# A list schedule of all tasks orders every engine; the first two batches' group sums are added on the chip

## The chip, the cores and the metric

The kernel runs on one core of one Trainium2 chip. The metric is the time of one execution in device microseconds; where several runs were made, the median is given with the lowest and the highest.

## What is computed

The reference is an attention block followed by a gated feed-forward block, in float32. There are 8 batches, 8 heads, 576 positions and 64 values a head; the feed-forward block has 512 inputs and 1536 inner columns.

```python
q_d = q.reshape(B, H, Sd, 4, D).mean(axis=3)        # and k_d, v_d: groups of four positions
out_up = np.repeat(softmax_attention(q_d, k_d, v_d), 4, axis=2)
mask = np.abs(pos[:, None] - pos[None, :]) < 4      # a band of 7 positions
out_local = softmax(where(mask, q @ k.T / 8, -1e9)) @ v
x = (out_up + out_local) as (4608 tokens, 512)
xn = x / sqrt(mean(x * x) + 1e-6) * rms_g
out = (silu(xn @ w_gate) * (xn @ w_val)) @ w_out
```

So each token gets a **coarse** attention over 144 group means, a **band** attention over its 7 neighbours, and the feed-forward block.

## The kernel before

**Chunks.** The 4608 tokens are cut into 18 chunks of 256. A chunk's band attention runs on 128 partitions. VectorE multiplies queries by a window of keys (`score`, line 387) and sums over the head's 64 values (`score_sum`, line 393), in 8 pairs a chunk; then a small softmax (lines 403 to 430). The weights multiply the values on three engines: ScalarE (line 441), VectorE and GpSimd, called POOL in the profile (both line 450). Seven products are summed by VectorE (line 470) or, in chunks 0 and 1, by TensorE with products against an identity matrix (line 465). `load_up` and `add_up` (lines 479 and 487) read the coarse result from device memory and add it. Squares (ScalarE, line 493), a sum over partitions (TensorE, line 500) and a Newton iteration (VectorE at lines 521 to 523 in chunks 0 and 1, else POOL at 525 to 528) give the norm, which line 532 multiplies in. TensorE transposes (line 543), ScalarE takes the high part `xh` (line 545), VectorE the low part `xl` (line 549).

**Feed-forward.** The weights and activations are held as a high and a low part, and every product is three: high x high, low x high, high x low. `Inner` makes for each of 12 column groups f the gate and the value product (24 products of 256 columns, line 619), a tanh on ScalarE (line 625), two steps on VectorE (lines 628 and 633), the high part `hs` on ScalarE (line 638) and its low part (line 641), on POOL in chunks 0 and 1 and on VectorE after. `second` (line 600, six products of 512 columns) follows two f later (`LAG = 2`) and adds up in `ps_o`.

**Coarse items.** There are 64 heads, of which two make one `Coarse` item: 32 items, 8 for each pair of batches. Scores (line 264), a maximum (273), exponentials (281), transposes (293), copies (298), products with the values (303), a scaling (318), and a store to device memory (319). A chunk needs the 8 items of its pair of batches. The sums over groups of four positions are made by transfers: `sum_loads` loads the first addend and lets POOL issue three more for each of `qk` and `vs` with `accum_op=ALU.add` (line 237), each of which waits for the one ahead.

**Weight decoding.** The weights arrive as 64-bit values, in 36 pieces of 512 KB (line 161), since the host only reinterprets the arrays. Each piece goes through `scale` (ScalarE, line 165), `last_bits` (POOL at 175 or ScalarE at 173), `join` (VectorE, line 182), the high part (ScalarE, lines 190 and 192) and `split`, the low part (VectorE at 204, POOL at 200). The 24 pieces of the gate and value weights and 12 of the output weights go through four buffers `o_sb`. All this belongs to the opening and to chunk 0.

**What sets the order.** Until chunk 0 is done, generators ("lanes") yield times to a rough clock (`Clock`), and `run` takes the lane that is due: this order holds on VectorE, POOL and SyncE. From chunk 1 on, a list `todo` of steps with a place (f from 0 to 12) is worked off between the f of the chunk ahead; `COARSE` says how many coarse items go with a chunk (0, 4, 3, 1, then 2). TensorE and ScalarE get their order from the framework's own scheduler.

Of the kernel before, what the change touches and what calls it, by code (L numbers as in the profile page):

```python
# [86 lines left out]
def attn_moe_kernel(  # L87
# [131 lines left out]
    latest = []  # L219


    up_dram = {}
    sums = {}

    def sum_loads(b, half, engine=nc.sync):
        if b == 1:
            qk = xp.tile([P, 2, 2, SD], FP32, name=("xh", "xl")[half])
            vs = ffn.tile([HALF, 4, 2, D], FP32, name="hs", bufs=LAG + 1)
        else:
            qk = glob.tile([P, 2, 2, SD], FP32, name="qk")  # L230
            vs = glob.tile([HALF, 4, 2, D], FP32, name="vs")
        sums[b, half] = (qk[:, 0], qk[:, 1], vs)
        steps = []
        for j in range(FAC):
            for t, src in ((qk.rearrange("p t h n -> p (t h n)"), qk_sum), (vs.rearrange("p h c d -> p (h c d)"), v_sum)):
                if j:
                    steps.append(lambda t=t, src=src[b, j, :, half]: nc.gpsimd.dma_start(out=t, in_=src, accum_op=ALU.add))  # L237
# [831 lines left out]
```

## Time and profile before

| what | value |
|---|---|
| median of 3 runs (lowest to highest) | 1182.68 us (1181.16 to 1185.43) |
| the profiled execution | 1189.22 us |
| its span, first to last instruction | 1187.4 us |
| its mean granted TensorE clock | 0.957 |
| read from device memory, written | 106.33 MB, 11.80 MB |

Times in rows are microseconds from the span's start. A row of the timeline gives start, duration, engine, line, operation, the tiles (output <- inputs), shapes and count, and in brackets how long the engine was idle just before and what ended that. Rows by stage give for each engine the busy time and the number of instructions, then TensorE's granted clock (1.00 is full), the transfer engines' mean busy share and what they moved in GB/s. Groups by line give count, busy time, mean duration in ns, and idle time ahead. PE is TensorE, PEld its weight load, DVE VectorE, ACT ScalarE, SP SyncE; a q behind a name is the engine's sequencer. A product of float32 operands stands in the trace as two records, one of the rounded type `fp32r` as one.

### The profile page before, as it was taken

How to read it: one execution, taken by the hardware profiler on the slowest of the kernel's cores; microseconds unless marked ns; L12 is line 12 of the kernel's file. 1: busy time of each engine (PE TensorE's matmuls, PEld its weight loads, DVE VectorE, ACT ScalarE, POOL GpSimd, SP SyncE). 2: the span in 40 equal slices, each digit the busy share in tenths (PEclk: the TensorE clock that was granted, in tenths of full speed). 3: DMA queues.
4: the chain of work that ended last, by engine and by line, in shares of the span. 5: the costliest groups of instructions: out<-in, count | busy, mean ns of one | idle time of the engine just before them, and what ended most of it. 6: DMA issues, size and time to landing. Idle time of an engine off the chain costs nothing. (4 is left out here: it accounts for less than half of the span.)

```text
span 1187.4 us, 22113 instructions
## 1 busy us (share of the span) xinstructions
PE 1105.9 (93%) x7940; PEld 1015.3 (86%) x7940; DVE 905.0 (76%) x1732; ACT 610.1 (51%) x2233; POOL 306.5 (26%) x503
## 2 busy tenths in 40 slices
PE   1893996987999999999999999999999999999998
PEld 1683995887999998989898989899999999999997
DVE  5676888976878878787878787888897979886322
ACT  0455762536372846473737374747374563727221
POOL 3443745533132112222222222211112121111000
PEclk9557897998999999999999999999999999999999
DMA  9946638555635252525252525222221313220000
GB/s 246 231 144 184 225 125 181 128 114 110 129 76 121 69 122 72 123 76 119 75 121 79 116 78 118 80 64 78 57 86 54 102 43 104 60 62 19 1 19 18
DMA packets 77293, 119.56 MB, mean 101 GB/s; under 512 B 27264, under 2 KB 36736, under 8 KB 77184
## 3 DMA queue, kind: packets, MB, share of 16 engines
q1 hardware_dynamic: 47760, 91.12, 26.5%
q0 software_dynamic: 11520, 21.24, 11.0%
q10 hardware_dynamic: 17904, 5.80, 2.1%
q8 instruction: 62, 1.02, 0.4%
q14 instruction: 47, 0.39, 0.1%
HBM read 106.33 MB, written 11.80 MB: 99 GB/s over the span
## 5 line engine op out<-in xcount | busy, mean ns | idle before, releaser
L600 PE MATMUL ps_o<-wo,hs 128*128 128x512 f32 x1296 | 366.6, 403 | 17.6 <-POOL hs L641 7.9
L619 PE MATMUL ps_h<-xh,wg 128*128 128x256 f32 x1728 | 360.4, 286 | 6.6 <-DVE sil L633 5.8
L619 PE MATMUL ps_h<-xh,wv 128*128 128x256 f32 x1728 | 351.1, 283 | 1.0 <-DVE wv L204 1.0
L619 PEld LDWEIGHTS ps_h<-xh,wg 128*128 128x128 f32 x1728 | 288.4, 192 | 17.8 <-DVE sil L633 6.4
L619 PEld LDWEIGHTS ps_h<-xh,wv 128*128 128x128 f32 x1728 | 286.8, 192 | 4.4 <-DVE wv L204 1.2
L441 ACT ACTIVATE prod<-kv,sc 128x64 f32<-128x64 f32 x1024 | 271.1, 406 | 22.5 <-DVE sc L430 11.1
L600 PEld LDWEIGHTS ps_o<-wo,hs 128*128 128x128 f32 x1296 | 223.7, 191 | 56.9 <-POOL hs L641 10.4
L619 PE MATMUL ps_h<-xl,wg 128*128 128x256 f32 x864 | 247.7, 287 | 0.3 <-DVE xl L549 0.3
L619 PE MATMUL ps_h<-xl,wv 128*128 128x256 f32 x864 | 245.2, 284 | 0.0
L625 ACT ACTIVATE sil<-ps_h 128x256 f32<-128x256 f32 x216 | 82.6, 382 | 245.8 <-PE ps_h L619 238.0
L450 POOL TENSOR_TENSOR prod<-sc,kv 128x256 f32<-128x256 f32 x144 | 116.5, 848 | 252.2 <-ACT xh L545 63.7
L619 PEld LDWEIGHTS ps_h<-xl,wg 128*128 128x128 f32 x864 | 165.5, 192 | 8.3 <-DVE sil L628 1.2
L619 PEld LDWEIGHTS ps_h<-xl,wv 128*128 128x128 f32 x864 | 165.7, 192 | 1.8
L628 DVE SCALAR_TENSOR_TENSOR sil<-sil,ps_h 128x256 f32<-128x256 f32 x216 | 90.0, 417 | 99.2 <-ACT sil L625 98.7
L387 DVE TENSOR_TENSOR prod<-q_t,kv 128x896 f32<-128x896 f32 x140 | 156.3, 1118 | 7.4 <-DMA q_t<-in_q_band_dram 7.1
L638 ACT ACTIVATE hs<-sil 128x256 fp32r<-128x256 f32 x216 | 88.9, 414 | 136.7 <-DVE sil L633 121.5
L470 DVE TENSOR_REDUCE x_t<-prod 128x128 f32<-128x896 f32 x128 | 136.8, 1084 | 26.8 <-ACT prod L441 13.3
L393 DVE TENSOR_REDUCE sc<-prod 128x14 f32<-128x896 f32 x144 | 154.3, 1077 | 0.0
L641 DVE TENSOR_TENSOR hs<-sil,hs 128x256 fp32r<-128x256 f32 x192 | 80.7, 421 | 31.8 <-ACT hs L638 31.8
L237 POOL DMA_DIRECT2D qk<-in_qk_sum_dram x42 | 37.7, 898 | 224.5 <-DMA qk<-in_qk_sum_dram 165.0
L633 DVE SCALAR_TENSOR_TENSOR sil<-sil,ps_h 128x256 f32<-128x256 f32 x216 | 89.6, 415 | 2.0
L450 DVE TENSOR_TENSOR prod<-sc,kv 128x128 f32<-128x128 f32 (+3 forms) x144 | 75.2, 554 | 3.4 <-PE ps_o L465 2.3
(111 smaller groups left out, 1016.6 us busy)
## 6 DMA issues: line engine op xcount, KB each, us to landing
kv<-in_k_pad_dram SPq DMA_DIRECT2D x72, 320.0 KB
kv<-in_v_pad_dram SPq DMA_DIRECT2D x72, 320.0 KB
qk<-in_qk_sum_dram POOLq DMA_DIRECT2D x42, 288.0 KB, 5.6
out_dram<-o_sb SPq DMA_DIRECT2D x36, 256.0 KB
q_t<-in_q_band_dram SPq DMA_DIRECT2D x70, 128.0 KB
vs<-in_v_sum_dram POOLq DMA_DIRECT2D x42, 144.0 KB, 3.9
wg<-in_w_gate_dram SPq DMA_DIRECT2D x8, 512.0 KB
wg<-in_w_val_dram SPq DMA_DIRECT2D x8, 512.0 KB
```

What stands on the lines that cost most here:

```text
L387: engine.tensor_tensor(out=pr[:, :, a:b], in0=bcast(q[:, s0:s0 + 2], 2, b - a), in1=window(k, s0, a, b), op=ALU.mult,)
L393: nc.vector.tensor_reduce(out=self.sc[:, j, par, s0:s0 + 2], in_=self.pr[i], axis=AX.X, op=ALU.add,)
L441: nc.scalar.activation(out=pr[:, o, s], in_=self.v[j, par][:, s0 + s + o], func=AF.Copy, scale=p[:, s, o:o + 1],)
L450: engine.tensor_tensor(out=self.pr[i][:, a:b], in0=bcast(p[:, :, a:b].rearrange("p s o -> p o s"), 3, D), in1=window(self.v[j, par], s0, a ...
L470: nc.vector.tensor_reduce(out=self.x[j][:, s0:s0 + 2, par], in_=pr.rearrange("p o s d -> p s d o"), axis=AX.X, op=ALU.add,)
L600: nc.tensor.matmul(out=o_ps[c][j], lhsT=lhs[:, cols], rhs=rhs(f)[:, 0], start=(f == 0 and i == 0), stop=(f == NF - 1 and i == 2),)
L619: nc.tensor.matmul(out=hp_[:, t], lhsT=wi(f)[:, 0, k], rhs=xi[:, k], start=(n == 0), stop=(n == 3 * KT - 1),)
L625: nc.scalar.activation(out=self.sil, in_=hp_[:, 0], func=AF.Tanh, scale=0.5)
L628: nc.vector.scalar_tensor_tensor(out=self.sil, in0=self.sil, scalar=1.0, in1=self.p[:, 0], op0=ALU.add, op1=ALU.mult,)
L633: nc.vector.scalar_tensor_tensor(out=self.sil, in0=self.sil, scalar=0.5, in1=self.p[:, 1], op0=ALU.mult, op1=ALU.mult,)
L638: nc.scalar.activation(out=self.hh, in_=self.sil, func=AF.Copy)
L641: (nc.gpsimd if self.c in REST_P else nc.vector).tensor_tensor(out=self.hl, in0=self.sil, in1=self.hh, op=ALU.subtract,)
```

## The change

**A list schedule.** All work becomes tasks with an engine (or a choice of two), a cost, a due time, the tasks that go ahead and the buffers that are allocated and used. `Plan.run` keeps a clock for each engine; it takes the task that can start first, and among those of one engine that could start within 0.15 us the one with the earliest due time, emits it, and goes on. Buffers count: a task that allocates waits until the users of the buffer that it takes over are done in the plan. The order so found holds on all five engines, TensorE and ScalarE included. `due` gives chunk 0 the time 70, chunk 1 125, chunk 2 180, and then 57 or 52 for each.

**Sums on the chip.** For the first two batches all four addends are loaded side by side with plain transfers into places where weights come later (`OpeningSums`). TensorE adds the four of `qk` with products against the identity into PSUM, ScalarE copies them out; POOL or VectorE adds those of `vs`. The other batches keep the accumulating transfers (`Sums`), each issue now a task of its own on POOL.

**Also.** The low part of `hs` may go to VectorE or POOL in every chunk, whichever the plan finds earlier. Coarse stores and loads are all issued by ScalarE. Coarse items are spread by due times: those of batches 2 and 3 over chunks 1 to 3, of 4 and 5 over chunks 4 to 8, of 6 and 7 over chunks 9 to 12. The first products for warming are 30 in place of 32. Raw weight pieces use eight places of the later gate and value weights rather than four, and four of the output weights.

```diff
+    def run(self):
...
+                for t in tasks:
+                    at = self.room(t) if t.allocs else 0.0
+                    if at is not None:
+                        floor = free["DMA"] - 3.0 if t.dma else 0.0
+                        found.append((max(free[e], t.at, at, floor), t))
...
+                first = min(s for s, _ in found)
+                pick = min(
+                    ((next(o for o in t.options if o[0] == e)[2], t.n, s, t) for s, t in found if s <= first + NEAR),
+                    key=lambda x: x[:2],
+                )
+                if best is None or pick[2] < best[0]:
+                    best = (pick[2], e, pick[3])
...
+    due = [70.0, 125.0, 180.0]
+    for c in range(2, NCH):
+        due.append(due[-1] + (57.0 if c < 12 else 52.0))
...
+    class Sums:
...
+            for j in range(1, FAC):
+                for i in range(2):
+                    done[i] = task(
+                        "POOL", ISSUE, lambda i=i, j=j: self.more(i, j), at - 30 + 5 * j, [done[i]],
+                        uses=[(self.qk_buf, self.vs_buf)[i]], dma=(0.288, 0.144)[i] * MB * 1.7,
+                    )
...
+    class OpeningSums:
...
+            for t in range(2):
+                p = buf(tag)
+                add = task("PE", 2.3, lambda t=t: self.add(t), at, got[:1], allocs=[p])
...
+            for j in range(1, FAC):
+                last = task(
+                    (("POOL", 1.5, at + 10), ("DVE", 0.7, at + 10)), 0, lambda e, j=j: self.add_v(j, e), at, [last],
+                    allocs=[self.vs_buf] if j == 1 else [], uses=[self.vs_buf],
+                )
...
+        def load_qk(self):
+            self.raw_qk = self.places[0].first_place()[:, :FAC * 4 * SD].rearrange("p (j x) -> p j x", j=FAC)
+            nc.sync.dma_start(out=self.raw_qk, in_=qk_sum[self.b, :, :, self.half].rearrange("j p x -> p j x"))
...
+        def add(self, t):
+            n = 2 * SD
+            self.p = self.pool.tile([P, n], FP32, name=self.tag)
+            for j in range(FAC):
+                nc.tensor.matmul(
+                    out=self.p, lhsT=ident_sb, rhs=self.raw_qk[:, j, t * n:(t + 1) * n], start=(j == 0), stop=(j == FAC - 1),
+                )
...
+        def copy(self, t):
...
+            nc.scalar.copy(out=self.qk[:, t].rearrange("p h n -> p (h n)"), in_=self.ps[t])
...
+        def add_v(self, j, engine):
...
+            (nc.gpsimd if engine == "POOL" else nc.vector).tensor_tensor(
+                out=vs, in0=self.raw_v[:, 0] if j == 1 else vs, in1=self.raw_v[:, j], op=ALU.add,
+            )
...
+                low = task(
+                    (("DVE", 0.42, soon), ("POOL", 0.95, soon)), 0, lambda e, f=f: self.low(f, e), soon, [high], uses=[sil, hs],
+                )
+                last = task(
+                    "PE", 1.375, lambda f=f: self.second(f), at + 4.2 * LAG, [low, last, *second_weights(f)],
+                    allocs=o_bufs if f == 0 else [], uses=[hs, *o_bufs],
+                )
...
-    with tc.manual_schedule(engines={mybir.EngineType.DVE, mybir.EngineType.Pool, mybir.EngineType.SP}):
...
+    with tc.manual_schedule():
+        plan.run()
```

What the plan makes of it is seen in the order of the instructions. **TensorE, the first instructions.** Before: products that only warm the engine (line 724), then scores, transposes and value products of the coarse items.

```order
L724 MATMUL ps_o<-hs 128x256 x20
L264 MATMUL ps_a<-qk 72x144 x4
L264 MATMUL ps_h<-qk 72x144 x4
L724 MATMUL ps_o<-hs 128x256 x2
L293 MATMUL ps_a<-ident_sb,a_g 72x72 x8
L293 MATMUL ps_h<-ident_sb,a_g 72x72 x4
L303 MATMUL ps_a<-vs,a_g 72x64 x4
```

After, with line 998 for warming, 395 for the additions against the identity, 459, 487 and 501 for the coarse item:

```order
L998 MATMUL ps_o<-hs 128x256 x21
L395 MATMUL ps_a<-wo_0_113,ident_sb 128x288 x8
L998 MATMUL ps_o<-hs 128x256 x5
L395 MATMUL ps_h<-wo_0_138,ident_sb 128x288 x8
L459 MATMUL ps_a<-qk 72x144 x4
L395 MATMUL ps_a<-wv_0_171,ident_sb 128x288 x4
L459 MATMUL ps_h<-qk 72x144 x4
L487 MATMUL ps_a<-ident_sb,a_g 72x72 x8
L395 MATMUL ps_a<-wv_0_171,ident_sb 128x288 x4
```

Sixteen additions stand ahead of the first scores, and the others between the items.

**VectorE, from the last coarse output of the opening on.** Before (318 is that output, 204 a weight's low part, 182 a join, 450 band products):

```order
L318 TENSOR_TENSOR o_g<-ps_o,z_g 72x256
L204 SCALAR_TENSOR_TENSOR wv_0_94<-o_sb,g_sb,wv_0_93 128x4x128
L182 SCALAR_TENSOR_TENSOR o_sb<-o_sb,wg_1_332 128x512
L450 TENSOR_TENSOR prod<-sc,kv 128x512
L182 SCALAR_TENSOR_TENSOR o_sb<-o_sb,wg_1_335 128x512
L204 SCALAR_TENSOR_TENSOR wg_0_92<-o_sb,g_sb,wg_0_91 128x4x128
L450 TENSOR_TENSOR prod<-sc,kv 128x512
```

After (514 is the output, 666 and 670 a score pair of chunk 1, 265 a join, 289 a low part, 754 the addition of the coarse result):

```order
L514 TENSOR_TENSOR o_g<-ps_h,z_g 72x256
L670 TENSOR_REDUCE sc<-prod 128x14
L265 SCALAR_TENSOR_TENSOR o_sb<-o_sb,wg_1_295 128x512
L265 SCALAR_TENSOR_TENSOR o_sb<-o_sb,wg_1_337 128x512
L666 TENSOR_TENSOR prod<-q_t,kv 128x896
L289 SCALAR_TENSOR_TENSOR wg_0_409<-o_sb,g_sb,wg_0_408 128x4x128
L289 SCALAR_TENSOR_TENSOR wv_0_416<-o_sb,g_sb,wv_0_415 128x4x128
L754 TENSOR_TENSOR x_t<-ps_o,up_t 128x512 x2
```

The band products of chunk 0, which stood behind the last coarse output, now all stand ahead of it.

**POOL, in a chunk with accumulating transfers.** Before (237 issues an accumulation, 450 are band products, 525 to 528 the Newton steps):

```order
L450 TENSOR_TENSOR prod<-sc,kv 128x2x128 x6
L237 DMA qk<-in_qk_sum_dram 128x576 x3
L237 DMA vs<-in_v_sum_dram 72x512 x2
L525 TENSOR_TENSOR newton<-rinv 128x8
L526 TENSOR_TENSOR newton<-newton,rms 128x8
```

After (349 issues an accumulation, 720 are band products, 891 the low part of `hs`):

```order
L349 DMA qk<-in_qk_sum_dram 128x576
L891 TENSOR_TENSOR hs<-sil,hs 128x256
L720 TENSOR_TENSOR prod<-sc,kv 128x2x128
L349 DMA vs<-in_v_sum_dram 72x512
L720 TENSOR_TENSOR prod<-sc,kv 128x2x128 x2
L349 DMA qk<-in_qk_sum_dram 128x576
L349 DMA vs<-in_v_sum_dram 72x512
L720 TENSOR_TENSOR prod<-sc,kv 128x2x128 x2
L349 DMA qk<-in_qk_sum_dram 128x576
L891 TENSOR_TENSOR hs<-sil,hs 128x256
```

The accumulations, which stood three in a row, have other work between them, and low parts stand directly behind some.

More of the change, by code (lines that the diff above doesn't have):

```diff
@@ L217, in load_second @@
         return load_weight(w_out[f * P:(f + 1) * P], wo, f, 1, None, None)
[L219 to L237, printed above, removed]
-                else:
-                    engine.dma_start(out=t, in_=src[b, j, :, half])
-        return steps
@@ L242, in load_sums @@
-    def load_sums(b, half):
-        for s in sum_loads(b, half):
-            s()
-    class Coarse:
-        def __init__(self, b, hp, pool, tag):
-            self.b, self.hp, self.pool, self.tag = b, hp, pool, tag
+    plan = Plan({
+        "qk": 2, "vs": 2, "a_g": 4, "o_g": 2, "m_g": 3, "z_g": 3, "kv": 4, "q_t": 2, "prod": 2, "sc": 2, "x_t": 2,
+        "up_t": 2, "xh": 2, "xl": 2, "sil": 3, "hs": LAG + 1, "o_sb": W_BUFS, "ps_h": 3, "ps_o": 2, "ps_a": 3,
+        "rms": 1, **{f"first{i}": 1 for i in range(8)}, **{f"second{i}": 1 for i in range(4)}, "stage": 1,
+    })
@@ L287, in values, with copy @@
+        def copy(self, par):
+            nc.scalar.copy(out=self.a[par], in_=self.t[par])
         def values(self):
[L288 to L298 removed]
@@ L395, in score_sum, with peak @@
             )
-        def edges(self):
+        def peak(self):
             sc = self.sc
@@ new lines, in first_weights @@
+    def first_weights(f):
+        return [whole[place[0, f // 4 * 8 + i]] for i in range(8)]
+    nc.scalar.dma_start(out=ident_sb, in_=ident)
+    nc.scalar.dma_start(out=min_sb, in_=band_min)
+    nc.scalar.dma_start(out=g_sb, in_=rms_g)
+    nc.scalar.dma_start(out=same_sb, in_=same_tok)
+    coarse = [(b, hp) for b in range(B) for hp in range(KT)]
+    opening = [
+        Coarse(*it, 15.0 + 4.0 * n, *((ps_h, "ps_h") if n // 2 % 2 else (ps_a, "ps_a"))) for n, it in enumerate(coarse[:2 * KT])
+    ]
@@ new lines, in attn_moe_kernel @@
+    atts = [Attention(0, 1, 2, (ps_o, "ps_o"), "DVE")]
+    atts.append(Attention(
+        1, 2, 2, (ps_a, "ps_a"), "DVE", [h.valued for h in opening] + atts[0].turns,
+    ))
+    for p_, (t0, t1) in enumerate(((due[1] + 10, due[4] - 30), (due[4], due[9] - 35), (due[9], due[13] - 35))):
+        n = 2 * KT * (p_ + 1)
+        for i, it in enumerate(coarse[n:n + 2 * KT]):
+            Coarse(*it, t0 + (t1 - t0) * i / 7, after=atts[1].added if p_ == 0 else ())
+    for c in range(2, NCH):
+        atts.append(Attention(c, {2: 2, 3: 3}.get(c, 4)))
```

1033 lines of the change are left out of this document (475 added, 558 removed).

## The prediction

> **What bounds the kernel now.** I read the page, then the trace by stages, then the waits inside the opening.
>
> The page's first part says which engine is full.
>
> ```profile
> PE 1105.9 (93%) x7940; PEld 1015.3 (86%) x7940; DVE 905.0 (76%) x1732; ACT 610.1 (51%) x2233; POOL 306.5 (26%) x503
> ```
>
> An average says little here, so I cut the span where the first product of line 619 of a 256-token chunk starts. Chunk 0 starts at 118.58 and the last one, chunk 17, at 1129.19 (rows further down). The stages are: the opening, chunks 0, 1, 2 and 3, then chunks 4 to 11, 12 to 16, and 17.
>
> ```profile
> core 0: us, PE busy (x) PEld busy (x) DVE busy (x) ACT busy (x) POOL busy (x), PEclk, DMA share, GB/s
> 0.00:118.60 118.60, 69.42 (x411) 58.80 (x411) 78.40 (x143) 49.87 (x155) 47.07 (x53) 0.71 0.77 201
> 118.60:185.80 67.20, 64.33 (x465) 61.18 (x466) 56.84 (x87) 42.87 (x110) 41.77 (x42) 0.95 0.49 162
> 185.80:276.10 90.30, 73.15 (x517) 63.71 (x516) 71.47 (x121) 35.98 (x135) 43.55 (x60) 0.91 0.66 141
> 276.10:342.90 66.80, 63.57 (x463) 58.65 (x461) 52.93 (x107) 35.73 (x141) 17.44 (x32) 0.92 0.48 104
> 342.90:396.90 54.00, 54.00 (x396) 50.44 (x396) 45.84 (x89) 30.31 (x119) 14.56 (x26) 1.00 0.49 107
> 396.90:868.50 471.60, 466.77 (x3473) 427.66 (x3472) 377.63 (x765) 266.50 (x1033) 98.87 (x196) 1.00 0.37 91
> 868.50:1129.20 260.70, 260.70 (x1852) 244.81 (x1851) 206.12 (x390) 136.68 (x517) 43.27 (x96) 1.00 0.21 59
> 1129.20:1187.50 58.30, 53.98 (x373) 50.08 (x371) 15.80 (x38) 12.18 (x29) 0.00 (x0) 0.99 0.05 19
> ```
>
> From 343 us on TensorE never rests and its clock is full. Chunks 12 to 16 hold no coarse item: 260.7 / 5 = 52.1 us each. Chunks 4 to 11 hold two: 471.6 / 8 = 58.95, so a coarse item costs (58.95 - 52.1) / 2 = 3.4 us. No order of the instructions takes that away. What is not such a floor lies ahead of 343 us: the opening, 118.6 us, in which VectorE works 78.4 and no chunk runs, and chunk 1, 90.3 us with 17 of TensorE idle.
>
> The opening's rows show what it waits for.
>
> ```profile
> 29.48 1.06 PE L264 MATMUL ps_a<-qk 64*72 64x144 f32 x8 [3.79 <-DMA qk<-in_qk_sum_dram]
> ...
> 50.44 1.23 PE L264 MATMUL ps_o<-xh 64*72 64x144 f32 x4 [5.00 <-DMA xh<-in_qk_sum_dram]
> ...
> 95.41 1.83 PE L465 MATMUL ps_o<-prod,ident_sb 128*128 128x128 f32 x14 [0.55 <-DVE prod L450]
> ...
> 111.45 0.60 PE L500 MATMUL ps_a<-ss,same_sb 128*128 128x8 f32 x2 [7.43 <-ACT up_t L493]
> 115.79 1.97 PE L543 MATMUL ps_a<-ident_sb,x_t 128*128 128x128 f32 x8 [3.74 <-DVE x_t L532]
> ```
>
> ```profile
> 118.58 0.80 PE L619 MATMUL ps_h<-xh,wg 128*128 128x256 f32 x2 [0.82 <-ACT xh L545]
> ```
>
> ```profile
> 1129.19 0.28 PE L619 MATMUL ps_h<-xh,wg 128*128 128x256 f32 x1
> ```
>
> The coarse scores wait until 29.5 and 50.4 us for sums that the accumulating transfers build. The tail is a chain: in the next two fences, SyncE stores the last coarse output at 84.4, loads it back only at 101.8, and VectorE adds it at 106.75; from there to the first product are 11.8 us.
>
> ```profile
> 84.37 0.32 SPq L319 DMA_DIRECT2D up<-o_g  x1
> ...
> 101.81 2.45 SPq L479 DMA_DIRECT2D up_t<-up  x4
> ```
>
> ```profile
> 6.50 2.09 DVE L387 TENSOR_TENSOR prod<-q_t,kv 128x896 f32<-128x896 f32 x2 [6.50 <-DMA q_t<-in_q_band_dram]
> ...
> 106.75 1.29 DVE L487 TENSOR_TENSOR x_t<-ps_o,up_t 128x512 f32<-128x512 f32 x2 [1.44 <-DMA up_t<-up]
> ```
>
> **The floor behind the opening.** 17 chunks x 52.1 + the last 58.3 + 24 coarse items x 3.4 + chunk 1's value sums on TensorE (8 x 1.83 by the row at 95.41 = 14.6) = 1041 us. Now it is 1187.4 - 118.6 = 1069. The excess of 28 is nearly all chunk 1: 90.3 - 52.1 - 4 x 3.4 = 24.6. The change removes no product of the floor.
>
> **The opening, part by part.** *Sums.* Twelve accumulating pairs leave the opening; four plain pairs of loads bring all four addends. The queues' rows give their price: accumulating q0 11.0% for 21.24 MB, plain q1 26.5% for 91.12.
>
> ```profile
> q1 hardware_dynamic: 47760, 91.12, 26.5%
> q0 software_dynamic: 11520, 21.24, 11.0%
> ```
>
> That is 6.1 us a MB against 3.45. The sizes stand in the page's last part:
>
> ```profile
> kv<-in_k_pad_dram SPq DMA_DIRECT2D x72, 320.0 KB
> ...
> qk<-in_qk_sum_dram POOLq DMA_DIRECT2D x42, 288.0 KB, 5.6
> ...
> q_t<-in_q_band_dram SPq DMA_DIRECT2D x70, 128.0 KB
> vs<-in_v_sum_dram POOLq DMA_DIRECT2D x42, 144.0 KB, 3.9
> wg<-in_w_gate_dram SPq DMA_DIRECT2D x8, 512.0 KB
> ```
>
> The first two heads need 4 x (320 + 128) KB of band loads and 4 x 288 of sums, 3.0 MB: at 201 GB/s (opening row) 15 us, at 1 / 3.45 = 290 GB/s 10. All four groups and the v loads make 10.2 MB: 35 to 51 us, where now even the third group is waited for until 50.4. *Their addition* is new: 32 products of 288 columns against the identity. The row at 95.41 has 7 of 128 columns in 1.83, 0.26 each; by columns 0.59, so 19 us of TensorE (38 at half clock), beside transfers that it would wait for. Twelve additions of v go to POOL (7) and VectorE (5 x 0.84, the nearest row below). *Stores and loads* of the coarse outputs go from SyncE's queue to ScalarE's: 8 stores x 0.32 and 8 loads x 0.61 by the rows above, 7.5 us, which ScalarE has (49.87 of 118.6 busy); uncovered, it would cost that. Coarse scores are the same products in another order: nothing.
>
> *VectorE* up to chunk 0's first product, by the two orders: three score pairs fewer, one join and one split fewer, one softmax of chunk 1 fewer; five additions and one low part more.
>
> ```profile
> L182 DVE SCALAR_TENSOR_TENSOR o_sb<-o_sb,wg 128x512 uint32<-128x512 uint32 x24 | 20.2, 853 | 0.5 <-POOL wg L175 0.5
> L204 DVE SCALAR_TENSOR_TENSOR wg<-o_sb,g_sb,wg 128x512 fp32r<-128x512 f32 x12 | 11.1, 922 | 5.7 <-ACT wg L192 5.7
> ...
> L450 DVE TENSOR_TENSOR prod<-sc,kv 128x384 f32<-128x384 f32 x8 | 6.9, 876 | 0.0
> L450 DVE TENSOR_TENSOR prod<-sc,kv 128x512 f32<-128x512 f32 x8 | 6.7, 840 | 2.3 <-PE ps_o L465 2.3
> ```
>
> ```profile
> L387 DVE TENSOR_TENSOR prod<-q_t,kv 128x896 f32<-128x896 f32 x111 | 120.4, 1085 | 0.2
> ...
> L393 DVE TENSOR_REDUCE sc<-prod 128x14 f32<-128x896 f32 x111 | 119.1, 1078 | 0.0
> ...
> L628 DVE SCALAR_TENSOR_TENSOR sil<-sil,ps_h 128x256 f32<-128x256 f32 x170 | 70.9, 417 | 49.2 <-ACT sil L625 48.9
> ```
>
> ```profile
> 95.27 0.69 DVE L182 SCALAR_TENSOR_TENSOR o_sb<-o_sb,wg 128x512 uint32<-128x512 uint32 x1
> ```
>
> A pair is 1.085 + 1.078 = 2.16. So 78.4 - 3 x 2.16 - 0.85 - 0.92 - 1.2 + 4.2 + 0.7 = 74 us. It starts at 6.5 as now. Its idle time is the unknown: it has 40 now; none would give 80.5. I take 14: 8 for the first sums and for TensorE between items, 6 in the tail, which stays (11.8 us from add to product; 2.45 to issue the loads, 2.5 to land, and an estimate of 3 for the store), while the order puts a score pair, joins and splits beside it. Chunk 0 then starts at 6.5 + 74 + 14 = **95**; bounds 86 and 110.
>
> **Chunks 0 to 2.** In chunk 0 VectorE has 22 joins x 0.853, 15 splits x 0.922, 8 products x 0.876, 6 pairs x 2.16, 24 gates x 0.417, 5 low parts x 0.42 and some 8 us of small ones: 73 us. TensorE has 52.1 + 14.6 = 66.7. So VectorE leads and costs 6, and a slow clock at the start about 4, as in the 0.95 of the stage row: 10 in all. These durations are means of the decoding stretch; some joins ran in 0.69 (row above), and at such prices chunk 0 would be TensorE's 66.7 and the sum 6 less.
>
> [...]
>
> In chunk 1 the order leaves two coarse items of four, and 45 us of VectorE work by the rows above against 52.1 + 2 x 3.4 = 59 of TensorE; the 24.6 of excess goes to nothing. What hides it is chunk 2's scores, begun in chunk 0; without that cover up to 24 come back. Later chunks are the floor.
>
> **POOL.** 129 low parts stand on POOL, 24 before; 25 of them directly behind an accumulating transfer, and the second product (two f later) waits for them.
>
> ```profile
> 196.54 1.22 PE L600 MATMUL ps_o<-wo,hs 128*128 128x512 f32 x2 [3.67 <-POOL hs L641]
> ```
>
> ```profile
> 193.90 0.92 POOL L237 DMA_DIRECT2D qk<-in_qk_sum_dram  x1 [5.76 <-DMA qk<-in_qk_sum_dram]
> ...
> 195.34 1.15 POOL L641 TENSOR_TENSOR hs<-sil,hs 128x256 fp32r<-128x256 f32 x1
> ```
>
> I take nothing for it: products of two f, some 8.7 us (52.1 / 12 each), stand between, more than the 5.76 that POOL was held here, and planned spacing puts other work where three accumulations now follow each other.
>
> **Sum.** 95 + 1041 + 10 = 1146 of span. The profiled execution took 1189.22, its span 1187.4; the median of three, 1182.68, is 4.7 below the span. So 1146 - 4.7 = 1141; I say **1140**.
>
> **Rivals.**
>
> *TensorE's clock holds the opening* (15%, of which 3% all the way). Between 29 and 80 us the eight coarse items ran at half clock although TensorE was busy.
>
> ```profile
> 29.00:80.00 51.00, 44.45 (x269) 35.93 (x269) 35.19 (x79) 26.23 (x98) 18.38 (x18) 0.51 0.77 193
> ```
>
> With these 44, 19 for the additions and 15 for the values at full clock, begun at 12, TensorE ends at 90 and chunk 0 starts 20 later, at 110: median 1156. With everything at half clock, 44 + 38 + 29 = 111, it ends at 123, starts at 143: 1194 - 5 = 1189, slower than before. It decides for slower once TensorE's opening work ends after 116 us. Against it: outside that stretch the opening's clock was (0.71 x 118.6 - 0.51 x 51) / 67.6 = 0.86, with the full 128x128 products of the value sums in it, and the additions are such products and now stand between the items.
>
> [...]
>
> *POOL's waits* (4%). If each of the 25 low parts behind an accumulation held TensorE for 3.67, as once at 196.5, that is 92 us: 1146 + 92 - 5 = 1233, slower. It decides from 12 such places, since the gain is 42.
>
> *Transfers* (10%). The eight weight pieces of f 8 to 11 land after 33.4 MB (35 x 512 KB, the sums, and the bands of chunk 0, chunk 1 and half of chunk 2); at 201 GB/s that is 166 us, and they are wanted at 95 + 44 = 139: 27 late, 1167. For it: this rate was measured. Against: it held accumulations at nearly twice the price.
>
> *The order does nothing* (3%): VectorE idles 40 as now (start 6.5 + 74 + 34 = 114) and the excess stays 28: 1183 - 5 = 1178, no change.
>
> **How the numbers follow.** The forecast has 68%. About 0.3%, 3.5 us, is what a measurement can tell. Faster: 68 + 12 + 10 = 0.90; no change 0.03; slower 3 + 4 = 0.07. The range goes from 86 + 1041 - 5 = 1122, less some 7 if coarse items interleave better than 3.4 each, so 1115, up past the transfers' 1167 to 1170; above it lie 0.10, below it less.
>
> **What would show it.** Right: chunk 0's first product near 95, chunk 1 near 60 us long, no chunk after it over 63, VectorE idle under 25 us before 95. Wrong: the opening's clock at 0.5 with TensorE busy after 70 us; waits of the second product for POOL's low part adding up to over 10 us; joins waiting for weight transfers in chunk 0.

## The result and the profile after

The changed kernel takes **1233.93 us** (median of 4 runs, 1230.71 to 1237.99); the kernel before, run beside it, 1184.06 (4 runs, 1181.16 to 1191.25). The ratio is 1.0414, 95% interval 1.0356 to 1.0471: slower by 4%, where faster by 4% was forecast. The profiled execution took 1234.64, with a span of 1232.8.

The first part of the page after. TensorE is busy longer than before (1126 against 1106) for the same chunks, and a smaller share of the span.

```profile
PE 1126.4 (91%) x8002; PEld 1014.2 (82%) x8002; DVE 911.5 (74%) x1633; ACT 637.6 (52%) x2247; POOL 378.7 (31%) x584
```

The stages after, cut as in the prediction where the first product of a chunk starts (line 867 now): the opening, chunks 0, 1, 2, then 3 to 11, 12 to 16, and 17. A chunk holds 288 products of this line and is taken to start when those of all chunks ahead have started; where two chunks mix, that is at most 1.5 us behind its own first product (2.8 in one run, `b_gate`).

```profile
0.00:103.70 103.70, 64.52 (x472) 53.83 (x472) 79.06 (x134) 52.71 (x163) 43.78 (x41) 0.84 0.87 265
103.70:185.20 81.50, 70.73 (x477) 65.09 (x478) 69.26 (x113) 49.31 (x121) 40.25 (x41) 0.93 0.58 143
185.20:250.80 65.60, 61.94 (x444) 55.60 (x443) 53.84 (x92) 27.76 (x98) 24.33 (x36) 0.97 0.40 95
250.80:314.80 64.00, 61.02 (x467) 55.33 (x466) 53.73 (x96) 32.62 (x123) 20.51 (x33) 1.00 0.37 91
314.80:896.20 581.40, 546.75 (x3906) 490.10 (x3904) 436.20 (x805) 313.08 (x1176) 178.09 (x298) 0.98 0.36 87
896.20:1174.10 277.90, 267.12 (x1873) 244.31 (x1872) 203.35 (x359) 149.80 (x540) 71.73 (x136) 1.00 0.22 61
1174.10:1232.80 58.70, 54.35 (x374) 50.00 (x372) 16.05 (x38) 12.28 (x29) 0.00 (x0) 1.00 0.05 19
```

Read the starts first. Chunk 0 starts 15 us earlier than before (103.7, 118.6), chunk 1 at the same time (185.2, 185.8), chunk 3 28 us earlier (314.8, 342.9). The loss lies behind: chunks 3 to 16 take 859.3 us, where they took 786.3. TensorE is busy 546.75 + 267.12 = 813.9 of them, so it stands idle 45.4; before it stood 4.8. Two coarse items more fall there, 19 for 17 (16 products each by the next rows, after and before), 2 x 3.4 = 7 us, which the earlier chunks saved.

```profile
L501 PE MATMUL ps_a<-vs,a_g 72*72 72x64 f32 x304 | 24.7, 239 | 0.0
```

```profile
L303 PE MATMUL ps_a<-vs,a_g 72*72 72x64 f32 x272 | 20.3, 227 | 0.0
```

What TensorE waited for in chunks 3 to 16, by line, with total, times and longest: first after, then the only row of before.

```profile
PE ps_h L867 <- DVE sil L877: 22.3, 27, 3.8
PE ps_a L815 <- DVE x_t L803: 6.1, 10, 1.0
PE ps_a L487 <- ACT a_g L478: 4.7, 11, 0.7
PE ps_h L867 <- ACT sil L874: 3.8, 7, 0.8
PE ps_o L902 <- POOL hs L891: 1.8, 2, 1.1
```

```profile
PE ps_o L600 <- DVE hs L641: 4.8, 6, 1.3
```

The first row is the find: TensorE's *first* products (line 867) wait for VectorE's *gate* step (line 877), though they use nothing that it makes. It reads the gate half of the PSUM tile `ps_h` into whose other half the value product (weights `wv`) is still to be written, and the order has it first. TensorE's order after, in chunk 12, with what each row waits for (Activation and DVE are the semaphores of ScalarE and VectorE):

```order
5008 L867 MATMUL ps_h<-xh,wg_0_409 128x256
5009 L902 MATMUL ps_o<-wo_0_440,hs 128x512 [waits Activation_49]
...
5015 L867 MATMUL ps_h<-xh,wv_0_415 128x256 [waits DVE_49]
```

A second product stands between the two halves of an f. The plan makes this itself: the value product comes `after` the gate product, so it is ready `HOP["PE"]` = 0.25 us past its end, and a product that could start at once has the first call, since only those within `NEAR` = 0.15 us are compared. Tanh and gate are then ready before the value product is taken up, and are emitted ahead of it. By the semaphores in the trace, 145 of 216 value products wait for VectorE so, 67 for ScalarE's tanh; before, 2 and 2.

In the plan, the gate step ends at the earliest 0.25 + 0.38 + 0.2 + 0.415 = 1.25 us after the gate products, less than a second product's 1.375. In the trace, for the 110 such value products of chunks 3 to 16, it ended 1.35 us after them in the median, 1.85 in the mean and 7.5 at most. 82 of the 110 started less than 0.6 us after the gate step had ended.

**One such wait in full.** VectorE, ScalarE and TensorE around 680 us, one fence each.

```profile
680.59 0.69 DVE L754 TENSOR_TENSOR x_t<-x_t,up_t 128x512 f32<-128x512 f32 x1 [4.52 <-DMA up_t<-up]
681.20 0.42 DVE L891 TENSOR_TENSOR hs<-sil,hs 128x256 fp32r<-128x256 f32 x1
681.53 0.42 DVE L877 SCALAR_TENSOR_TENSOR sil<-sil,ps_h 128x256 f32<-128x256 f32 x1
```

```profile
675.46 2.50 ACTq L748 DMA_DIRECT2D up_t<-up  x4
...
678.33 0.37 ACT L874 ACTIVATE sil<-ps_h 128x256 f32<-128x256 f32 x1
```

```profile
677.97 0.28 PE L867 MATMUL ps_h<-xh,wg 128*128 128x256 f32 x1
682.00 0.58 PE L867 MATMUL ps_h<-xh,wv 128*128 128x256 f32 x1 [3.76 <-DVE sil L877]
```

ScalarE issued four loads of coarse results until 678; VectorE stood 4.52 us at the addition that needs them; the gate step, whose tanh was done at 678.7, stood behind that addition; and TensorE stood 3.76 us for the gate. The clock then adds to it (windows of 1 us: TensorE busy, its records, granted clock, DMA share, GB/s).

```profile
680.00:681.00 1.00, 0.00 (x0) 1.00 1.02 184
681.00:682.00 1.00, 0.00 (x0) 0.50 0.60 75
682.00:683.00 1.00, 1.00 (x4) 0.50 0.65 107
...
687.00:688.00 1.00, 1.00 (x6) 0.59 0.28 62
688.00:689.00 1.00, 1.00 (x11) 1.00 0.06 13
```

After a wait of 3.8 us TensorE runs at half clock from 682 to about 687.8: 5.8 us at half speed, some 2.9 us more. At a mean of 0.98 over 581 us (stage row) the clock makes up about 12 of the 73, an estimate from that row.

So the 73 us are: 45.4 - 4.8 = 41 of idle, 7 of coarse items, 12 of clock, and 13 that no row of TensorE's products accounts for.

### The profile page after: what moved, and what is told of

Read it like the earlier page. It is cut to its first block, busy times and chain, and to the rows that moved or that the text cites. A ratio compares the mean times of both kernels' runs of the same rounds, so it can differ in the third digit from the quotient of the medians.

```text
span 1232.8 us, 22325 instructions
## 1 busy us (share of the span) xinstructions
PE 1126.4 (91%) x8002; PEld 1014.2 (82%) x8002; DVE 911.5 (74%) x1633; ACT 637.6 (52%) x2247; POOL 378.7 (31%) x584
## 4 chain that ended last, share of the span: by engine, by line
PE 61%; DVE 17%; DMA 7%; ACT 6%; issue 4%; POOL 4%; SPq 1%; ACTq 0%; DVEq 0%; POOLq 0%
PE ps_h L867 40%; PE ps_o L902 15%; DVE sil L877 3%; DVE prod L666 2%; ACT a_g L478 2%; DVE x_t L739 2%; DVE sc L670 2%; DMA wg<-in_v_sum_dram 2%; PE ps_a L501 2%; DMA qk<-in_qk_sum_dram 1%; DVE prod L720 1%; DMA up<-o_g 1%; DVE sil L882 1%; ACT prod L713 1%; DMA up_t<-up 1%
## 5 line engine op out<-in xcount | busy, mean ns | idle before, releaser
L867 PE MATMUL ps_h<-xh,wv 128*128 128x256 f32 x1728 | 358.2, 291 | 36.0 <-DVE sil L877 29.7
L867 PE MATMUL ps_h<-xh,wg 128*128 128x256 f32 x1728 | 343.3, 287 | 5.4 <-ACT wg L277 3.0
L902 PE MATMUL ps_o<-wo,hs 128*128 128x512 f32 x1296 | 344.3, 401 | 4.3 <-POOL hs L891 1.8
L867 PEld LDWEIGHTS ps_h<-xh,wg 128*128 128x128 f32 x1728 | 284.2, 194 | 9.9 <-ACT wg L277 3.2
L713 ACT ACTIVATE prod<-kv,sc 128x64 f32<-128x64 f32 x1024 | 274.8, 403 | 26.1 <-DVE x_t L739 14.0
L902 PEld LDWEIGHTS ps_o<-wo,hs 128*128 128x128 f32 x1296 | 231.5, 192 | 48.9 <-POOL hs L891 3.7
L891 POOL TENSOR_TENSOR hs<-sil,hs 128x256 fp32r<-128x256 f32 x129 | 109.8, 855 | 447.0 <-ACT hs L888 399.3
L877 DVE SCALAR_TENSOR_TENSOR sil<-sil,ps_h 128x256 f32<-128x256 f32 x216 | 90.0, 418 | 146.9 <-PE ps_h L867 104.3
L720 POOL TENSOR_TENSOR prod<-sc,kv 128x256 f32<-128x256 f32 x144 | 108.6, 778 | 154.1 <-DVE x_t L739 84.3
L720 DVE TENSOR_TENSOR prod<-sc,kv 128x128 f32<-128x128 f32 (+3 forms) x144 | 85.0, 595 | 0.3
L764 ACT ACTIVATE up_t<-x_t 128x128 f32<-128x128 f32 x144 | 44.5, 309 | 22.9 <-DVE x_t L754 17.8
```

Source lines behind the costliest of these rows:

```text
L713: nc.scalar.activation(out=self.pr[i][:, o, s], in_=self.v[j, par][:, s0 + s + o], func=AF.Copy, scale=p[:, s, o:o + 1],)
L720: (nc.vector if engine == "DVE" else nc.gpsimd).tensor_tensor(out=self.pr[i][:, a:b], in0=bcast(p[:, :, a:b].rearrange("p s o -> p o s"), ...
L867: nc.tensor.matmul(out=self.p[f][:, t], lhsT=wi(f)[:, 0, k], rhs=xi[:, k], start=(n == 0), stop=(n == 3 * KT - 1),)
L877: nc.vector.scalar_tensor_tensor(out=self.sil[f], in0=self.sil[f], scalar=1.0, in1=self.p[f][:, 0], op0=ALU.add, op1=ALU.mult,)
L891: (nc.gpsimd if engine == "POOL" else nc.vector).tensor_tensor(out=self.hs[f][:, 1], in0=self.sil[f], in1=self.hs[f][:, 0], op=ALU.subtract,)
L902: nc.tensor.matmul(out=self.o[j], lhsT=lhs[:, cols], rhs=rhs(f)[:, 0], start=(f == 0 and i == 0), stop=(f == NF - 1 and i == 2),)
```

## The experiments

Theory **T**: the value products wait for readers of their own tile, because the order puts those first. Rivals: **R1**, TensorE's costs in the plan are too small; **R2**, the low parts on POOL slow VectorE and TensorE; **T2**, every hand-over that the plan times too early is a stall in TensorE's fixed order, whichever line it is. All kernels but the one so marked are the changed kernel with the edit shown; ratios are against the kernel before, with 95% intervals. "Chunks 3 to 16" is the time between the starts of chunks 3 and 17.

| run | median us | ratio (95%) | chunk 0 starts | chunk 1 | chunk 3 | chunks 3 to 16 | of it TensorE idle |
|---|---|---|---|---|---|---|---|
| before | 1184.06 | | 118.6 | 185.8 | 342.9 | 786.3 | 4.8 |
| changed | 1233.93 | 1.0414 (1.0356 to 1.0471) | 103.7 | 185.2 | 314.8 | 859.3 | 45.4 |
| v_next | 1233.12 | 1.0394 (1.0355 to 1.0434) | 103.0 | 196.3 | 327.8 | 843.6 | 40.6 |
| g_after | 1190.00 | 1.0024 (1.0001 to 1.0048) | 106.8 | 189.0 | 311.0 | 818.3 | 24.9 |
| t_after | 1188.17 | 1.0009 (0.9987 to 1.0031) | 108.7 | 199.4 | 318.1 | 810.0 | 20.4 |
| tv | 1180.31 | 0.9944 (0.9925 to 0.9962) | 104.3 | 186.4 | 311.5 | 809.7 | 17.9 |
| pe_cost | 1254.75 | 1.0593 (1.0539 to 1.0646) | 104.2 | 186.1 | 325.4 | 870.6 | 55.0 |
| low_dve | 1233.10 | 1.0387 (1.0346 to 1.0429) | 105.4 | 186.0 | 314.0 | 859.8 | 47.7 |
| hop | 1244.88 | 1.0486 (1.0447 to 1.0526) | 116.0 | 201.1 | 328.3 | 860.5 | 47.8 |
| g_hop | 1216.14 | 1.0244 (1.0200 to 1.0289) | 110.8 | 191.3 | 310.4 | 843.2 | 39.3 |
| g_free2 | 1258.01 | 1.0610 (1.0566 to 1.0654) | 110.2 | 190.5 | 320.0 | 882.9 | 51.7 |
| t_acc | 1196.61 | 1.0094 (1.0060 to 1.0127) | 142.7 | 203.2 | 326.4 | 807.1 | 19.0 |
| t_turn | 1186.39 | 0.9988 (0.9964 to 1.0011) | 104.7 | 195.9 | 319.2 | 807.5 | 18.6 |
| **t_late** | **1167.35** | **0.9845 (0.9818 to 0.9872)** | 105.3 | 187.6 | 310.2 | 799.1 | 12.7 |
| tv_late | 1184.96 | 1.0007 (0.9979 to 1.0036) | 106.8 | 187.4 | 312.5 | 811.3 | 18.4 |
| tl_low | 1212.26 | 1.0236 (1.0196 to 1.0276) | 105.8 | 188.0 | 311.3 | 841.7 | 43.7 |
| b_gate (kernel before) | 1197.77 | 1.0126 (1.0070 to 1.0183) | 119.7 | 186.9 | 341.3 | 796.2 | 10.9 |

### Taking the wait away: g_after, t_after, v_next, tv

g_after:

```diff
-                gate = task("DVE", 0.415, lambda f=f: self.gate(f), soon, [tanh], uses=[hp, sil])
+                gate = task("DVE", 0.415, lambda f=f: self.gate(f), soon, [tanh, val], uses=[hp, sil])
```

> The gate step on VectorE is made to follow the value product of the same f in the plan; the two products of an f may still stand apart on TensorE. One of the 216 groups of value products waits for VectorE in the order, against 145. T, if the wait itself and not the distance of the two halves is the cause: 1165 to 1190, close to the run in which the value product follows directly. If the distance costs by itself (a PSUM tile held longer): 1200 to 1235. R1, R2: 1215 to 1240.

t_after, in which tanh waits too:

```diff
-                tanh = task("ACT", 0.38, lambda f=f: self.tanh(f), soon, [first], allocs=[sil], uses=[hp])
                 val = task("PE", 1.375, lambda f=f: self.first(f, 1), at, [first], uses=[hp, *x])
+                tanh = task("ACT", 0.38, lambda f=f: self.tanh(f), soon, [val], allocs=[sil], uses=[hp])
```

> The tanh of an f follows its value product in the plan, as it did in the kernel before, so neither ScalarE nor VectorE reads the PSUM tile while the value product is still to come: 4 groups of value products wait for another engine in the order, against 214 in the changed kernel, 206 with the gate step alone moved, and 4 in the kernel before. Theory T (the value products' waits for readers of their tile): the 10 us that line 867 still waits for line 874 in the run with the gate step moved go too: 1170 to 1190. Theory T2 (TensorE's fixed order waits at every hand-over that the plan timed too early, whichever line it is): as with the gate step moved or a little worse, 1180 to 1205, with the waits on other lines.

1190 and 1188: 44 and 46 us back, and chunks 3 to 16 go from 859 to 818 and 810. The first lies at the upper end of T's range; the second lies in T's and in T2's, so it doesn't tell the two apart. TensorE's waits between 300 and 1180 us in g_after and then in t_after: the row of line 877 is gone in both, that of line 874 in the second, and what is left stands on other lines, as T2 has it.

```profile
PE ps_a L815 <- DVE x_t L803: 10.3, 10, 2.6
PE ps_h L867 <- ACT sil L874: 10.1, 8, 3.0
PE ps_h L867 <- DVE xl L823: 1.5, 1, 1.5
```

```profile
PE ps_a L815 <- DVE x_t L803: 11.6, 9, 3.7
PE ps_o L902 <- POOL hs L891: 4.2, 4, 1.9
```

Of the 49 us by which chunks 3 to 16 are shorter in t_after than in the changed kernel, 41 come with the gate step and 8 with tanh, which is no more than such plans differ by (t_late below). The second brings the whole time next to nothing, since chunk 0 takes 90.7 us in place of 82.3. So the wait for VectorE was the dearer one. Of its 41 us, 20.5 are idle time of TensorE and as many its busy time (813.9 to 793.4), in which the clock has, by estimate, some 7 (mean granted 0.984 and 0.992). So the 13 us that no row accounts for go with this wait too; where they lie isn't shown.

v_next, which takes out the planner's gap, and tv, which is v_next and t_after together:

```diff
-                val = task("PE", 1.375, lambda f=f: self.first(f, 1), at, [first], uses=[hp, *x])
+                val = task("PE", 1.375, lambda f=f: self.first(f, 1), at, with_=[first], uses=[hp, *x])
```

> Theory T (the value products of an f wait on VectorE): in the changed kernel the plan counts 0.25 us between the gate product and the value product of one f although both are TensorE's, puts another product between them, and the gate step, which reads the same PSUM tile, comes ahead of the value product in the order; 145 of 216 groups of value products then start with a wait for VectorE. Here the value product may start in the plan when the gate product starts, so it follows directly and 27 such waits are left. T: the 22 us (TensorE) that line 867 waits for line 877 between 315 and 1174 us go, with the slow clock behind the longer ones (13 us) and the stalls inside the products; of the 73 us lost after chunk 3, 50 to 70 come back: 1165 to 1185. Rival R1 (TensorE's costs in the plan are too small, so the plan drifts from what runs): 1215 to 1240, since the costs stay. Rival R2 (low parts on POOL slow VectorE and TensorE): 1225 to 1240.

> Tanh after the value product, and the value product directly behind the gate product, as the kernel before emits them; 2 groups of value products wait for another engine. Theory T: nothing is left to gain from that, 1180 to 1195. If the halves standing together cost by themselves, which would explain why the run with that edit alone took 1233 though its waits for VectorE's gate step fell from 22 to 6 us: 1210 to 1240.

v_next missed T's range: 1233 lies in those of R1 and R2, which the next section tests. It won 16 us in chunks 3 to 16 (843.6) and lost 13 ahead of them: chunk 0 took 93.3 us in place of 81.5, and chunk 3 began at 327.8 in place of 314.8. Its first rows of waits say in part why it won no more: line 877 fell to 6.1, but 52 value products still wait for VectorE or ScalarE in the order, and other lines took over.

```profile
PE ps_a L771 <- ACT up_t L764: 11.8, 11, 3.5
PE ps_a L815 <- DVE x_t L803: 9.6, 17, 1.2
PE ps_h L867 <- DVE sil L877: 6.1, 9, 2.9
```

tv, the same with tanh behind the value product, took 1180, and chunks 3 to 16 34 us less than in v_next and as long as in t_after (809.7 and 810.0). So halves that stand together cost nothing by themselves; that 52 such waits cost 34 us is more than their rows show, and how the rest arises is not settled.

### The rivals: pe_cost, low_dve, hop, g_hop, g_free2

```diff
-                    "PE", 1.375, lambda f=f: self.first(f, 0), at, [*att.turned, *weights(f)], allocs=[hp], uses=x,
+                    "PE", 1.44, lambda f=f: self.first(f, 0), at, [*att.turned, *weights(f)], allocs=[hp], uses=x,
```

(and the same for the value product and `second`)

> Only the costs of TensorE's three tasks of an f in the plan go from 1.375 to 1.44 us, near what twelve products take in the trace; 149 groups of value products still wait for VectorE. R1: the plan follows the chip better and most of the 73 us come back, 1170 to 1195. T: the waits stay, 1215 to 1245.

R1 falls: 1255, worse than the changed kernel, outside both ranges. A reason could be that, with a slower TensorE in the plan, results of the other engines stand still earlier in its order; that was not tried by itself.

low_dve:

```diff
-                    (("DVE", 0.42, soon), ("POOL", 0.95, soon)), 0, lambda e, f=f: self.low(f, e), soon, [high], uses=[sil, hs],
+                    (("DVE", 0.42, soon), ("POOL", 0.95, soon)) if c < 2 else "DVE", 0.42,
+                    lambda e="DVE", f=f: self.low(f, e), soon, [high], uses=[sil, hs],
```

> From chunk 2 on all low parts of the hidden values stand on VectorE, as in the kernel before; nothing else is changed. R2: VectorE's and TensorE's operations are no longer slowed by POOL, and 40 us or more come back, 1170 to 1195. T: the value products still wait for the gate step, and VectorE has some 100 x 0.42 = 42 us more to do ahead of the gates: 1230 to 1270.

R2 falls as it was stated: 1233, chunks 3 to 16 859.8 against 859.3. The edit also gives VectorE some 42 us more to do, so a smaller cost of POOL's low parts could be hidden in this.

hop, and g_hop, which is g_after with it:

```diff
-HOP = {"PE": 0.25, "ACT": 0.2, "DVE": 0.15, "POOL": 0.2, "SP": 0.0}
+HOP = {"PE": 0.25, "ACT": 0.8, "DVE": 0.8, "POOL": 0.8, "SP": 0.0}
```

> The plan's time from the end of a task of ScalarE, VectorE or POOL to the start of one that waits for it goes from 0.15 to 0.2 us to 0.8 us: results are put later in the order of the engines that use them, TensorE's above all. The gate step stays ahead of the value product; 100 groups of value products wait for VectorE in the order. T: 1215 to 1240, since most of those waits stay. T2: the order leaves room for what the chip takes longer than the plan, and 30 us or more come back: 1165 to 1205.

> Both edits: the gate step after the value product, and 0.8 us from an engine's end to its user. T: about the 1190 of the gate step alone, 1180 to 1200. T2: better than either alone, 1150 to 1180, with TensorE's waits between 300 and 1180 us under 10 us.

Both went the wrong way, hop by 11 us against the changed kernel and g_hop by 26 against g_after, and both lie above what either theory gave them. T2 in the form "more slack helps" falls; slack also makes the opening longer (chunk 0 at 116.0 and 110.8).

g_free2 is g_after with this:

```diff
-    with tc.manual_schedule():
+    with tc.manual_schedule(engines={mybir.EngineType.DVE, mybir.EngineType.Pool, mybir.EngineType.SP}):
```

> The gate step after the value product, and the plan's order held only on VectorE, POOL and SyncE; TensorE and ScalarE get theirs from the framework's scheduler, as in the kernel before. T2, if the order on TensorE itself is what costs: 1140 to 1175. If the order of VectorE (which work it does ahead of the gate steps) is what costs, and TensorE only waits for that: 1180 to 1210, no better than the gate step alone.

1258, far above both ranges. TensorE's waits between 300 and 1180 us in it:

```profile
PE ps_h L867 <- DVE sil L882: 20.9, 17, 3.1
PE ps_o L902 <- ACT hs L888: 14.3, 13, 2.9
```

The framework's order of TensorE does not fit the plan's order of VectorE: gate products wait for a PSUM tile that the product step (line 882) still reads, second products for `hs`. So letting TensorE and ScalarE go while the plan's order of VectorE stays brings nothing back; the fixed order on TensorE is not the cause by itself. The same tasks with no order held were not tried.

### The wait alone, in the kernel before: b_gate

From chunk 1 on, tanh and gate are issued between the two halves:

```diff
-            self.sil = ffn.tile([P, C], FP32, name="sil", bufs=3)
-            nc.scalar.activation(out=self.sil, in_=hp_[:, 0], func=AF.Tanh, scale=0.5)
+                if t == 0 or self.c == 0:
+                    if t == self.c == 0:
+                        continue
+                    self.sil = ffn.tile([P, C], FP32, name="sil", bufs=3)
+                    nc.scalar.activation(out=self.sil, in_=hp_[:, 0], func=AF.Tanh, scale=0.5)
+                    if self.c:
+                        self.step()
...
```

> The kernel before, with one thing changed from chunk 1 on: the tanh and the gate step of an f are issued between its gate and its value product, not after both. 206 groups of value products then wait for VectorE in the order, against 2. Theory T (the wait for the gate step costs by itself): slower, 1215 to 1260, with line 619 waiting for line 628's step for 20 us and more. Rival (the wait only costs where the plan has fixed TensorE's order; the framework's scheduler puts other products there): 1180 to 1198.

The rival's range held: 1198, 12 us slower, of which 10 in chunks 3 to 16. Its waits there name no first product at all:

```profile
PE ps_o L600 <- DVE hs L650: 5.5, 2, 4.2
PE ps_a L543 <- DVE x_t L532: 5.4, 4, 2.2
```

The trace shows why: in chunks 3 to 16 of b_gate a value product starts 5.5 us (median) after its gate products end, with other products in between, and the gate step is done after 2.7; only 4 of 168 start less than 0.6 us after it. In the changed kernel those that wait for VectorE start after 2.3 us, and 82 of 110 that close behind the gate step. So the same wait on 206 value products costs 12 us in an order that puts this much work in between, while taking it out of the plan's order brought 44 to 46. T is true only in that form: the wait, and an order of VectorE and TensorE that doesn't allow for it.

### The opening: t_acc

t_after, with the first two batches' sums built by accumulating transfers again:

```diff
-                sums[b, hp // 2] = Sums(b, hp // 2, at) if b > 1 else OpeningSums(b, hp // 2, self.pool, tag)
+                sums[b, hp // 2] = Sums(b, hp // 2, at)
```

> Tanh after the value product, as in the run of that edit, and the first two batches' sums built by accumulating transfers again, as in the kernel before; all else of the plan stays. If the sums on the chip carry the gain ahead of chunk 3: chunk 0 begins 8 to 15 us later than the 108.7 of that run, 1194 to 1206. If the list schedule alone carries it: 1183 to 1192, chunk 0 within 4 us of 108.7.

1197, in the first range, but not in the way it said. The opening and chunk 0 of t_acc, then of t_after:

```profile
0.00:142.70 142.70, 63.88 (x423) 53.15 (x423) 110.46 (x184) 79.41 (x206) 72.61 (x76) 0.62 0.92 251
142.70:203.20 60.50, 60.50 (x460) 57.76 (x459) 44.06 (x80) 23.28 (x79) 19.43 (x23) 1.00 0.35 75
```

```profile
0.00:108.70 108.70, 69.84 (x472) 58.19 (x472) 77.01 (x135) 52.69 (x163) 38.87 (x41) 0.77 0.86 253
108.70:199.40 90.70, 74.92 (x514) 68.95 (x515) 82.32 (x131) 51.45 (x132) 40.36 (x41) 0.88 0.58 147
```

Chunk 0 begins 34 us later and takes 30 less, since VectorE has then done 110 us of its work: 35 of the 36 joins of the decoding stand ahead of chunk 0, against 14 in t_after. What an early chunk 0 wins is nearly all given back while VectorE and ScalarE decode beside it: 3.8 us are left at chunk 1, 8.3 at chunk 3, 8.4 in the medians.

### What is left: t_turn, t_late, tv_late, tl_low

t_turn is t_after with

```diff
-                norm = task("DVE", 0.69, lambda j=j: self.norm(j), T - 8, [root], uses=[xs[j]])
+                norm = task("DVE", 0.69, lambda j=j: self.norm(j), T - 8, [root], uses=[xs[j]], lag=2.5)
```

> Tanh after the value product, and in the plan 2.5 us from the end of the norm step (line 803) to the transposes that use it (line 815), in place of 0.15. T2 for this one hand-over: TensorE's 11.6 us of waits at line 815 go, 1172 to 1184. If the plan's slack doesn't bear on it, because VectorE runs later than the plan by more, or the wait only changes its place: 1184 to 1200.

The wait at line 815 leaves the list and the time stays (1186, t_after 1188): it has only changed its place. TensorE's first rows from 310 us on:

```profile
PE ps_a L771 <- ACT up_t L764: 4.9, 4, 1.6
PE ps_o L902 <- ACT hs L888: 4.2, 3, 2.9
PE ps_o L902 <- POOL hs L891: 3.7, 3, 2.6
```

t_late, then tv_late (t_late with the value product directly behind the gate product from chunk 1 on), then tl_low (t_late with the edit of low_dve):

```diff
-                tanh = task("ACT", 0.38, lambda f=f: self.tanh(f), soon, [val], allocs=[sil], uses=[hp])
+                tanh = task("ACT", 0.38, lambda f=f: self.tanh(f), soon, [val if c else first], allocs=[sil], uses=[hp])
```

> Tanh after the value product from chunk 1 on; in chunk 0 the order is built as in the changed kernel. In the run with the edit in every chunk, chunk 0 took 90.7 us with one wait of TensorE of 9.6 (line 487 for ScalarE's exponentials, which stood behind VectorE's score pairs); in the changed kernel 81.5. If that wait belongs to the edit: 1170 to 1182, faster than the kernel before. If it is one of several places at which the fixed order can stand, and another takes its place: 1183 to 1198.

> From chunk 1 on, tanh after the value product, and the value product directly behind the gate product. If standing together costs nothing, as in the run with both edits in every chunk (1180 there, 1188 with the halves free to stand apart): 1160 to 1172, like the 1167 of the run with tanh moved from chunk 1 on. If it costs: 1180 to 1215.

> Tanh after the value product from chunk 1 on, and all low parts on VectorE from chunk 2 on. If POOL's low parts slow VectorE's products (1.145 us at line 666 in the run with tanh moved, 1.085 in the kernel before) and hold TensorE at line 902 (up to 4 us in all), 5 to 15 us come back: 1152 to 1164, with line 666 back at 1.09. If they cost nothing, and VectorE's 100 x 0.42 us more stands ahead of gate steps: 1165 to 1185.

**t_late beats both kernels**: 1167, ratio 0.9845 (0.9818 to 0.9872), 3 us under its first range. Chunk 0 takes 82.3, as expected, 8 of the 21 us that it wins on t_after. Chunks 3 to 16 take 799.1, where the floor is 14 x 52.1 + 19 x 3.4 = 794; the 11 us won there were not foreseen, since from chunk 1 on the edit is the same, and are luck of the plan. tv_late came out as if standing together cost 18 us, some 12 of them in chunks 3 to 16. In every chunk (tv against t_after) the same edit won 8, all of it in chunk 0, and nothing in chunks 3 to 16. One edit with such different results means that this is not a cost of the edit: any change makes the plan another one, and with the waits gone such plans differ by 10 us and more in chunks 3 to 16.

tl_low, above both its ranges, lost 45 us against t_late, where 5 to 15 were to be won. 17 of them are one wait (the first row), with nothing amiss in POOL: VectorE, with more to do, ran six score pairs in a row (612.7 to 626 us) ahead of a maximum for which the exponentials, and behind them TensorE, stood. The rest isn't accounted for. VectorE's score products took less time there, with fewer low parts on POOL: 1106 ns in t_late and 1088 in tl_low, 2 us in all.

```profile
PE ps_a L487 <- ACT a_g L478: 19.5, 3, 17.1
```

```profile
L666 DVE TENSOR_TENSOR prod<-q_t,kv 128x896 f32<-128x896 f32 x107 | 118.3, 1106 | 0.2
```

```profile
L666 DVE TENSOR_TENSOR prod<-q_t,kv 128x896 f32<-128x896 f32 x108 | 117.5, 1088 | 0.1
```

## Why the prediction was wrong

**The step that failed** is "No order of the instructions takes that away", and its echo "Later chunks are the floor". The floor is a lower bound that TensorE keeps only while nothing in its queue waits, and the change fixed that queue anew for all 18 chunks. Chunks 3 to 16 took 859.3 against 794, 65 us of the miss. The order after showed value products that wait for VectorE, and the prediction read the order only at the opening, at chunk 1 and at POOL's low parts. Its own sign, no chunk over 63 us behind chunk 1, failed at once: chunk 3 took 70.6. The floor itself stands: t_late came within 5 us of it.

- *Opening*, forecast 95, bounds 86 to 110: 103.7. VectorE began at 5.5, not 6.5; its work was 79.1 where 74 was summed, and its idle time behind the start 19.1 where 14 was taken. Right in kind, 9 us short. The 3 us that the tail gave to the store are shown by no run; in the changed kernel the first load of chunk 0 (line 748) was issued at 87.64, 3.8 us after the issue of the last store ahead of it had ended (line 517, 83.56 + 0.30), and what it waited for isn't shown.
- *Chunk 0*, forecast 76.7: 81.5, so chunk 1 starts at 185.2, not at 172. VectorE's work was less than summed (69.3, not 73), but it stood 12, of which 9 for gate and value products of TensorE (6.3 at line 877, 2.9 at line 882), a wait that the sum had at nothing; t_acc shows that the stretch up to chunk 1 hardly depends on when chunk 0 starts.
- *Chunk 1*, forecast 59: 65.6. The excess of 24.6 went to 6.7; this is the gain that was real. *Chunk 2*, 62.3 by the floor with three coarse items: 64.0.
- *Sum*. Chunk 3 would start at 95 + 76.7 + 59 + 62.3 = 293 and did at 314.8: 22. With 65, 0.4 in chunk 17, and 6 since the median lay 1.1 above the span here and not 4.7 below, that is the 94 us between 1140 and 1234. In t_late chunk 3 still starts at 310.2, 17 us late, and the median stays 27 above the forecast: 17 of these 27 belong to the stages ahead of chunk 3, not to the step that failed.
- *POOL's waits*, a rival with 1233 us: the time is almost that, the mechanism isn't there. TensorE waited 1.8 us for POOL's low part in chunks 3 to 16. A rival's number that fits is no evidence; its row is.
- *TensorE's clock in the opening*: the stretch that ran at 0.51 ran at 0.94, with TensorE about as busy (42.4 of 51 us). That the products for warming raise the clock isn't shown: in the changed kernel 21 of them ran from 4.64 to 9.14 us, the clock was 1.00 up to 11 us, 0.50 from 12 to 18, and 1.00 again from 19 to 40, with the additions against the identity (line 395) running from 14.83 on.

```profile
29.00:80.00 51.00, 42.41 (x360) 35.82 (x359) 42.47 (x83) 36.95 (x126) 29.64 (x27) 0.94 0.96 307
```

- *Transfers*: the opening moved 265 GB/s where 201 was assumed, and VectorE's joins in chunk 0 waited for no weight piece (POOL stood 8.3 us for one, at line 258).
- *Score products and POOL's low parts*: the products (lines 387 and 666) took 1085 ns in the kernel before and 1124 in the changed one. At 106 of them that is 4 us. With the low parts back on VectorE (low_dve) they took 1082, at the same time of 1233 us; so what the low parts cost this group is not what the time hangs on. By what way they cost it isn't shown.

## What to carry to other kernels

A busy engine's time is a floor only for an order that feeds it. When a change replaces the order of all engines, look in the new order for every instruction of the bounding engine that waits for another engine and didn't before, above all for a writer that now stands behind the readers of its own tile's other half, and ask what can be queued ahead of it: 5.5 us of other products hid most of the wait in b_gate, 2.3 us did not in the changed kernel. A gain in the opening is worth what is left of it two stages later, not what it is at its end.

## What the runs showed of the hardware

After a wait of 3.8 us TensorE ran at half clock for 5.8 us of work (rows at 680 us above). The same was seen behind a dense run of short waits: in the next rows, four windows of 1 us in which it was busy 2.13 of 4 us, with no wait in the list over 1.0 us, were followed by 3 us at 0.50 to 0.57.

```profile
612.00:613.00 1.00, 0.46 (x4) 1.00 0.00 0
613.00:614.00 1.00, 0.58 (x4) 1.00 0.00 0
614.00:615.00 1.00, 0.68 (x5) 1.00 0.73 74
615.00:616.00 1.00, 0.41 (x3) 1.00 0.91 154
616.00:617.00 1.00, 1.00 (x7) 0.57 1.01 171
617.00:618.00 1.00, 1.00 (x7) 0.50 0.31 59
618.00:619.00 1.00, 1.00 (x4) 0.50 0.00 0
```

In the first case the half clock was granted from 681 us on, 2.8 us after TensorE's last product (677.97 + 0.28); in the second TensorE had been busy half of the time. What sets the granted clock isn't shown.
